# Turning two bf16 channels as one 4-byte element on VectorE, in a chunk attention followed by a multiplicative feed-forward layer

## The chip, the cores and the metric

One core of a Trainium2 chip runs the kernel. The time is the device's microseconds from start to end of one execution, and each figure is the median of several runs on one chip, except for the three single runs with other steps. Runs of one kernel lie within about 1% of each other. Each experiment is compared with runs of the kernel before beside it, on the same chip. All comparisons are of fast runs (in the single runs the state is unknown), and the profiled executions have the TensorE clock at 0.99 to 1.00 of full speed except where the text says otherwise.

## The reference, cut to what matters

```python
# q, k, v: (8, 8, 576, 64) float32: batch, heads, sequence, channels
q_c, k_c, v_c = (t.reshape(B, H, 9, 64, 64) for t in (q, k, v))       # chunks of 64
scores = matmul(q_c, k_c.transpose(0, 1, 2, 4, 3)) / sqrt(64)
attn = softmax(scores)
x = matmul(attn, v_c) -> (B * S, H * D) = (4608, 512)
h = ((x @ w1) * (x @ w2)) @ w3          # w1, w2: (512, 1024), w3: (1024, 1024)
out = h @ w_out                         # w_out: (1024, 512)
```

The kernel computes in bf16 with float32 sums, and multiplies w3 by w_out first.

## The kernel before

The 4608 tokens are 18 "pairs" of 256. For a pair, q and k have to be turned so that channels lie on partitions (T), scores are made (S), exponentials taken on ScalarE (E), multiplied by v (P), normalised (N), and the result x turned (X), again on VectorE. Then come the products with w1 and w2 (A, B), their product (C, M) and the last product (O). Two pairs share their A and B from pair 4 on. A list names the order of all these steps. W is the product of w3 (turned in V) and w_out. The kernel turns blocks of 32x32 on VectorE, so 64 channels of a head come to lie as two halves `e` on the same 32 partitions:

```python
def do_T(p, s, h=None):                                    # q (s=0) and k (s=1)
    nc.vector.transpose(
        qkT_t[g][:, :, p % 2, s].rearrange("p e h (y t) -> p h t e y", t=2),
        qk_t[p][:, s].rearrange("p h (t e y) -> p h t e y", t=2, e=2))

def do_G(g, a):                                            # pairs 8 to 17 alone: both halves
    for i in (0, 2, 1, 3):                                 # to 64 partitions, by DMA
        e = (i + a) % 2
        move(qkm_t[g][blk[i // 2 * 2 + e], i % 2], qkT_t[g][blk[i], e])

def do_S(p):
    for h in range(H):
        if p < 8:                                          # two sums over 32 channels: 64 matmuls
            for e in range(2):
                for i in range(4):
                    mm(s_t[p][...], lhsT=qkT_t[g][blk[i], e, m, 1, h, :],
                       rhs=qkT_t[g][blk[i], e, m, 0, h, :], start=(e == 0), stop=(e == 1))
        else:                                              # one sum over 64 channels: 32 matmuls
            for i in (0, 3, 1, 2):
                mm(s_t[p][...], lhsT=qkm_t[g][half[i // 2], i % 2, m, 1, h, :], rhs=..., ...)

def do_AB(p, j, f, which):
    rhs = new_xt(p // 2)[:].rearrange("p (s o t) -> p o s t", s=2, o=4)     # p >= 8
    for ki in range(4):
        mm(ps_t[p, j][:, which, ...], lhsT=w[:, ki, f * 128:(f + 1) * 128], rhs=rhs[:, ki], ...)
# ... (cut: loads, softmax, X, H, C, M, V, W, O, stores)
```

The softmax here doesn't subtract the row's maximum and nothing guards it: scores larger than these inputs give would overflow.

Of the kernel before, what the change touches and what calls it, by code (L numbers as in the profile page):

```python
# [14 lines left out]
M2.1 A2.2 N3.0 B2.2 C2.2 X3.0 A2.3 N3.1 B2.3 X3.1 C2.3 M2.2 S4 M2.3 A3.0 E4 B3.0 C3.0 A3.1 M3.0 B3.1  # L15
C3.1 V0 A3.2 M3.1 B3.2 C3.2 V1 A3.3 M3.2 B3.3 C3.3 V2 W0 M3.3 V3 W1 Z0 V4 V5 W2 Z1 V6 V7 T5.0 Z2 W3
T5.1 q10 k10 T6.0 T6.1 P4 v10 q11 k11 Z3 S5 N4.0 O0 E5 X4.0 N4.1 X4.1 T7.0 O1 T7.1 Y0 Q0 T8.0 P5 v11
q12 k12 Y1 S6 T8.1 O2 Q1 E6 N5.0 X5.0 N5.1 X5.1 O3 T9.0 T9.1 Y2 G4.0 P6 v12 q13 k13 A4.0 N6.0 B4.0
G4.1 Y3 X6.0 N6.1 C4.0 A4.1 X6.1 B4.1 C4.1 M4.0 Q2 S7 Q3 M4.1 A4.2 E7 T10.0 B4.2 C4.2 T10.1 P7 v13
q14 k14 A4.3 M4.2 B4.3 N7.0 C4.3 A4.4 X7.0 M4.3 B4.4 C4.4 N7.1 A4.5 M4.4 B4.5 C4.5 X7.1 S8 M4.5 S9  # L20
E8 A4.6 T11.0 B4.6 E9 T11.1 P8 v14 q15 k15 C4.6 A4.7 M4.6 G5.0 B4.7 C4.7 N8.0 A6.0 M4.7 B6.0 N8.1
C6.0 G5.1 A6.1 X8.0 B6.1 M6.0 C6.1 X8.1 P9 v15 A6.2 M6.1 N9.0 B6.2 C6.2 N9.1 A6.3 M6.2 B6.3 C6.3
X9.0 A6.4 M6.3 B6.4 C6.4 X9.1 A6.5 T12.0 H4.0 B6.5 C6.5 M6.4 A6.6 M6.5 B6.6 T12.1 H4.1 C6.6 S10 S11
M6.6 E10 A6.7 T13.0 B6.7 E11 P10 T13.1 C6.7 O4 M6.7 G6.0 N10.0 N10.1 X10.0 G6.1 P11 Y4 X10.1 O5
N11.0 N11.1 x11 q16 k16 v16 Q4 X11.0 X11.1 T14.0 A8.0 H5.0 Y5 B8.0 T14.1 C8.0 A8.1 M8.0 B8.1 H5.1
C8.1 T15.0 A8.2 B8.2 M8.1 C8.2 T15.1 Q5 A8.3 B8.3 C8.3 M8.2 G7.0 S12 M8.3 S13 E12 A8.4 T16.0 B8.4
E13 G7.1 P12 T16.1 C8.4 A8.5 B8.5 M8.4 C8.5 N12.0 A8.6 M8.5 B8.6 C8.6 N12.1 x12 q17 k17 v17 A8.7
M8.6 B8.7 C8.7 X12.0 P13 M8.7 A10.0 X12.1 B10.0 C10.0 N13.0 A10.1 M10.0 B10.1 N13.1 C10.1 A10.2
X13.0 B10.2 M10.1 C10.2 X13.1 S14 S15 M10.2 E14 A10.3 H6.0 T17.0 B10.3 E15 P14 T17.1 C10.3 A10.4
H6.1 M10.3 B10.4 C10.4 N14.0 A10.5 M10.4 B10.5 G8.0 C10.5 N14.1 A10.6 M10.5 B10.6 C10.6 X14.0 P15  # L30
G8.1 X14.1 A10.7 M10.6 B10.7 N15.0 C10.7 O6 N15.1 M10.7 X15.0 X15.1 H7.0 S16 Y6 S17 O7 E16 E17 H7.1
P16 Y7 O8 Q6 N16.0 Q7 N16.1 X16.0 X16.1 P17 Y8 A12.0 N17.0 Q8 B12.0 N17.1 C12.0 A12.1 X17.0 B12.1
M12.0 C12.1 X17.1 A12.2 M12.1 H8.0 B12.2 C12.2 A12.3 M12.2 B12.3 C12.3 H8.1 A12.4 M12.3 B12.4 C12.4
A12.5 M12.4 B12.5 C12.5 A12.6 M12.5 B12.6 C12.6 A12.7 M12.6 B12.7 C12.7 O9 M12.7 O10 Y9 Q9 A14.0 Y10
B14.0 C14.0 Q10 A14.1 M14.0 B14.1 C14.1 A14.2 M14.1 B14.2 C14.2 A14.3 M14.2 B14.3 C14.3 A14.4 M14.3
B14.4 C14.4 A14.5 M14.4 B14.5 C14.5 A14.6 M14.5 B14.6 C14.6 A14.7 M14.6 B14.7 C14.7 O11 M14.7 O12
Y11 Q11 A16.0 Y12 B16.0 C16.0 Q12 A16.1 M16.0 B16.1 C16.1 A16.2 M16.1 B16.2 C16.2 A16.3 M16.2 B16.3
C16.3 A16.4 M16.3 B16.4 C16.4 A16.5 M16.4 B16.5 C16.5 A16.6 M16.5 B16.6 C16.6 A16.7 M16.6 B16.7
C16.7 O13 M16.7 O14 Y13 Q13 O15 Y14 Q14 O16 Y15 Q15 Y16 Q16 O17
"""  # L40


# [1 line left out]
def kernel(  # L44
# [11 lines left out]
    nc = tc.nc  # L56
    B, H, S, D = q.shape
    P = 128
    BL = 32
    NB = P // BL  # L60
    CH = 64
# [3 lines left out]
    DF = moe_w1.shape[1]  # L65
    KO = DM // P
    FO = DF // P
    UT = 2 * CH
    PT = 2 * UT
# [6 lines left out]
    bf = mybir.dt.bfloat16  # L76
    f32 = mybir.dt.float32
# [5 lines left out]
    asb = ctx.enter_context(tc.tile_pool(name="asb", bufs=2))  # L83
    msb = ctx.enter_context(tc.tile_pool(name="msb", bufs=2))
    ps = ctx.enter_context(tc.tile_pool(name="ps", bufs=4, space=bass.MemoryType.PSUM))

    def inorder(ins):
        tc.keep_in_program_order(ins)
        return ins

    def mm(*a, **kw):
        return inorder(nc.tensor.matmul(*a, **kw))  # L92

    def load(dst, src):
        return inorder(nc.gpsimd.dma_start(dst, src))  # L95

    def psum(name):
        return ps.tile([P, 2, 512], f32, tag="p", name=name)


    w1 = wpool.tile([P, KO, DF], bf, name="w1")
    w2 = wpool.tile([P, KO, DF], bf, name="w2")

    w3 = wpool.tile([P, DF // BL, DF // NB], bf, name="w3")
    wo = wpool.tile([P, FO, DM], bf, name="wo")
# [20 lines left out]
    qk_t = {}  # L126
# [15 lines left out]
    def heads(h):  # L142
        return slice(0, H) if h is None else slice(h * HH, (h + 1) * HH)
# [31 lines left out]

    def load_wo():
        for i in range(NB):
            load(wo[i * BL:(i + 1) * BL],
                 moe_w_out[i * DF // NB:(i + 1) * DF // NB].rearrange("(k x) n -> x k n", x=BL))

    half = [slice(0, CH), slice(CH, P)]
    blk = [slice(i * BL, (i + 1) * BL) for i in range(NB)]
    qkT_t, qkm_t, s_t, e_t, pv_t, xn_t, xm_t, xt_t = {}, {}, {}, {}, {}, {}, {}, {}
# [7 lines left out]
    def do_T(p, s, h=None):  # L191


        g = p // 2
        if g not in qkT_t:
            qkT_t[g] = asb.tile([P, 2, 2, 2, H, CH], bf, tag="qkT", bufs=2, name="qkT")
        inorder(nc.vector.transpose(  # L197
            qkT_t[g][:, :, p % 2, s, heads(h)].rearrange("p e h (y t) -> p h t e y", t=2),
            qk_t[p][:, s, heads(h)].rearrange("p h (t e y) -> p h t e y", t=2, e=2)))
# [10 lines left out]
    def do_S(p, hh=None):  # L210
        g, m = divmod(p, 2)
        if p not in s_t:
            s_t[p] = psum("s_ps")
        for h in range(H)[heads(hh)]:
            if p < 8:
                for e in range(2):
                    for i in range(NB):
                        mm(s_t[p][half[i % 2], i // 2, h * CH:(h + 1) * CH],
                           lhsT=qkT_t[g][blk[i], e, m, 1, h, :], rhs=qkT_t[g][blk[i], e, m, 0, h, :],
                           start=(e == 0), stop=(e == 1))  # L220
            else:
                for i in (0, 3, 1, 2):
                    mm(s_t[p][half[i % 2], i // 2, h * CH:(h + 1) * CH],
                       lhsT=qkm_t[g][half[i // 2], i % 2, m, 1, h, :],
                       rhs=qkm_t[g][half[i // 2], i % 2, m, 0, h, :], start=True, stop=True)
# [35 lines left out]

    def new_xt(g):

        if g not in xt_t:
            xt_t[g] = asb.tile([P, KO * GT], bf, tag="xt", bufs=4, name="xt")
        return xt_t[g]

    def do_X(p, u):
        g, m = divmod(p, 2)
        if p < 8:  # L270
            t0 = m * PT + u * UT
            inorder(nc.vector.transpose(  # L272
                new_xt(g)[:].rearrange("p (o t) -> p o t", o=KO)[:, :, t0:t0 + UT]
                .rearrange("p o (m y) -> p m o y", y=BL),
                xn_t[p][:, u].rearrange("p r (c n) (z o) -> p (r c) o n z", c=2, o=KO)))
        else:

            if g not in xm_t:
                xm_t[g] = asb.tile([P, 2, KO, 2, UT], bf, tag="xm", bufs=2, name="xm")
            inorder(nc.vector.transpose(  # L280
                xm_t[g][:, u, :, m].rearrange("p o (c y) -> p c o y", y=BL),
                xn_t[p][:].rearrange("p u r m d -> p (u r) m d")[:, :, 2 * u:2 * u + 2]
                .rearrange("p c n (z o) -> p c o n z", o=KO)))

    def do_H(g, a):

# [4 lines left out]
    ab_t, ps_t, a_t, o_t = {}, {}, {}, {}  # L291
# [9 lines left out]
    def do_AB(p, j, f, which):  # L301

        if p >= 8:
            rhs = new_xt(p // 2)[:].rearrange("p (s o t) -> p o s t", s=2, o=KO)
        else:
            rhs = new_xt(p // 2)[:].rearrange("p (o t) -> p o t", o=KO)
            if p < 4:
                rhs = rhs[:, :, p % 2 * PT:(p % 2 + 1) * PT]
        fs = (f,) if p >= 4 else (2 * j, 2 * j + 1)
        n = GT // len(fs)  # L310
        for i, f in enumerate(fs):
            for ki in range(KO):
                mm(ps_t[p, j][:, which, i * n:(i + 1) * n],
                   lhsT=(w1, w2)[which][:, ki, f * P:(f + 1) * P], rhs=rhs[:, ki],
                   start=(ki == 0), stop=(ki == KO - 1))

    def do_A(p, j):
# [3 lines left out]
    def do_B(p, j):  # L321
        do_AB(p, j, j, 1)
# [55 lines left out]
    w3T_t = {}  # L378

    def do_V(f):  # L380
        w3T_t[f] = msb.tile([P, FO, P], bf, tag="w3T", bufs=4, name="w3T")
        inorder(nc.vector.transpose(
            w3T_t[f][:].rearrange("p k (f y) -> p f k y", y=BL),
            w3[:, NB * f:NB * (f + 1), :].rearrange("p f (k x) -> p f k x", x=BL)))

    def do_W(m):
        ps_t["w", m] = psum("w_ps")
        for i in range(2):
            w3T = w3T_t.pop(2 * m + i)
            for ki in range(FO):  # L390
                mm(ps_t["w", m][:, i, :], lhsT=w3T[:, ki, :], rhs=wo[:, ki, :],
                   start=(ki == 0), stop=(ki == FO - 1))

    def do_Z(m):
# [59 lines left out]
```

## Time and profile before

| | before |
|---|---|
| median | 245 us (244.5 to 245.5) |
| TensorE busy, share of the span | 93% |
| VectorE busy | 153.7 us |
| instruction packets of TensorE's queue | 21 |

A row of the table of groups by shape has line, engine, operation and tiles, then the count, busy us and mean ns of one, then idle time before. The mean ns of a matmul is its modelled duration and not its pace, as matmuls overlap: the first row has a mean of 379 ns, while the same matmuls follow one another every 216 ns. The pace is read from the chain or the timeline: a stretch divided by its count. These rows of the kernel before are the ones to compare with later, first the groups and then four pieces of the chain of waits (start us, us, what):

```profile
L92 PE MATMUL ab_ps<-xt,w 128*128 128x512 bf16 x441 | 99.2, 379 | 0.5
L92 PE MATMUL ab_ps<-xt,w 128*128 128x256 bf16 x240 | 27.6, 273 | 0.9 <-DVE xt L272 0.9
L92 PE MATMUL s_ps<-qkm 64*64 64x64 bf16 x320 | 3.6, 194 | 0.0
```

```profile
44.14 0.64 PE s_ps L92 x64
96.43 0.64 PE s_ps L92 x64
98.90 0.37 PE pv L92 x30
188.06 13.81 PE ab_ps L92 x64
```

The last line gives the pace of a 128x512 matmul of x: 13.81 us / 64 = 216 ns. The line at 96.43 us is the scores of two pairs, 32 matmuls each.

### The profile page before, as it was taken

The page shows a single profiled execution, that of the slowest core. Times are in us where ns is not written, and L with a number is a line of the kernel's source. Part 1 is how long each engine was busy: PE and PEld are TensorE (multiplying, and loading weights), DVE is VectorE, ACT ScalarE, POOL GpSimd, SP SyncE. Part 2 cuts the span into 40 slices and gives each one's busy share as a digit, 9 for nine tenths or more (in the row PEclk, how much of TensorE's full clock was granted, in tenths as well). Part 3 has the DMA queues.
Part 4 walks back from the last instruction along what each step waited for, and adds up shares of the span by engine and source line. Part 5 has one row for each costly group of instructions (what it writes and reads, how often), then busy time and mean ns, then how long its engine had stood idle before and what let it go on. Part 6 is the DMA issues. An engine that isn't in the chain of part 4 may idle for free.

```text
span 243.1 us, 6347 instructions
## 1 busy us (share of the span) xinstructions
PE 225.9 (93%) x2731; PEld 120.3 (49%) x2753; DVE 153.7 (63%) x232; ACT 85.1 (35%) x116; POOL 83.3 (34%) x112
## 2 busy tenths in 40 slices
PE   1299989999999979999999999999999999999994
PEld 1247868864545444444444444444444444444443
DVE  1856799689899578999998899918440332143000
ACT  2412323423333343534326335162332332332322
POOL 8847974665986444773260240000000000000000
PEclk9999999999999999999999999999999999999999
DMA  7999999999999999999999893735502200400244
GB/s 179 179 185 180 186 168 199 196 193 170 154 172 218 226 228 252 173 219 192 209 237 213 251 137 83 173 89 203 145 0 89 86 0 0 175 0 1 86 173 173
DMA packets 93595, 37.63 MB, mean 155 GB/s; under 512 B 75008, under 2 KB 86528, under 8 KB 93568
## 3 DMA queue, kind: packets, MB, share of 16 engines
q0 software_dynamic: 82592, 18.88, 83.9%
q1 hardware_dynamic: 9936, 17.83, 24.8%
q10 hardware_dynamic: 1040, 0.52, 0.8%
q8 instruction: 21, 0.34, 0.6%
q14 instruction: 6, 0.05, 0.1%
HBM read 38.80 MB, written 9.44 MB: 198 GB/s over the span
## 4 chain that ended last, share of the span: by engine, by line
PE 70%; DMA 16%; DVE 5%; SPq 3%; issue 2%; POOL 2%; ACT 0%; DVEq 0%; POOLq 0%
PE ab_ps L92 38%; PE o_ps L92 23%; PE w_ps L92 6%; DMA w<-in_moe_w_dram 4%; DMA qkm<-qkT 3%; DMA xt<-xm 3%; DMA qk<-in_k_dram 3%; DMA qk<-in_q_dram 3%; SPq L189 3%; PE s_ps L92 2%; PE pv L92 2%; DVE qkT L197 2%; DVE xn L260 1%; DVE ab L341 1%; POOL vbuf L95 1%
## 5 line engine op out<-in xcount | busy, mean ns | idle before, releaser
L92 PE MATMUL ab_ps<-xt,w 128*128 128x512 bf16 (+1 forms) x681 | 126.8, 342 | 1.4 <-DVE xt L272 0.9
L92 PEld LDWEIGHTS <-w 128*128 128x128 bf16 x704 | 67.3, 98 | 55.4 <-DVE xt L272 1.4
L341 DVE TENSOR_TENSOR ab<-a_sb,ab_ps 128x512 bf16<-128x512 f32 x71 | 47.8, 674 | 43.5 <-ACT a_sb L326 43.3
L326 ACT COPY a_sb<-ab_ps 128x512 f32<-128x512 f32 x71 | 41.6, 586 | 81.3 <-PE ab_ps L92 81.1
L92 PE MATMUL o_ps<-w3o,ab 128*128 128x512 bf16 (+1 forms) x285 | 63.3, 373 | 0.6
L197 DVE STREAM_TRANSPOSE qkT<-qk 128x1024 bf16<-128x1024 bf16 x36 | 45.1, 1289 | 8.0 <-ACT qk L140 5.5
L92 PEld LDWEIGHTS <-ab 128*128 128x128 bf16 x296 | 28.5, 98 | 32.3
L95 POOL DMA_DIRECT2D vbuf<-in_v_dram x40 | 33.9, 855 | 17.9 <-DMA qk<-in_k_dram 4.8
L371 ACT COPY o_sb<-o_ps 128x1024 f32<-128x1024 f32 x17 | 17.2, 1012 | 45.2 <-PE o_ps L92 41.3
L260 DVE TENSOR_TENSOR xn<-pv,rc 128x512 bf16<-128x512 f32 x36 | 24.9, 692 | 1.4
L95 POOL DMA_DIRECT2D qk<-in_q_dram x23 | 18.1, 790 | 9.9 <-DMA qk<-in_k_dram 3.1
L95 POOL DMA_DIRECT2D qk<-in_k_dram x23 | 18.0, 785 | 8.8 <-DMA vbuf<-in_v_dram 5.1
L230 ACT ACTIVATE e<-s_ps 128x1024 bf16<-128x1024 f32 x16 | 15.9, 1028 | 2.5 <-PE s_ps L92 2.2
L92 PE MATMUL w_ps<-wo,w3T 128*128 128x512 bf16 x62 | 13.9, 379 | 0.1
L280 DVE STREAM_TRANSPOSE xm<-xn 128x512 bf16<-128x512 bf16 x20 | 13.6, 697 | 0.2
L257 DVE RECIPROCAL rc<-pv 128x8 f32<-128x8 f32 x36 | 6.9, 192 | 9.9 <-PE pv L92 9.9
L95 POOL DMA_DIRECT2D w<-in_moe_w_dram x16 | 11.1, 697 | 5.8 <-DMA vbuf<-in_v_dram 2.3
L92 PEld LDWEIGHTS <-e 64*32 64x32 bf16 (+1 forms) x832 | 7.8, 97 | 8.5 <-issue 7.1
L272 DVE STREAM_TRANSPOSE xt<-xn 128x512 bf16<-128x512 bf16 x16 | 11.4, 711 | 0.5
L92 PE MATMUL pv<-vbuf,e 64*32 64x65 bf16 (+1 forms) x832 | 10.2, 198 | 1.5 <-ACT e L230 1.1
L92 PEld LDWEIGHTS <-qkT 32*64 32x64 bf16 x512 | 5.5, 117 | 11.0 <-DVE qkT L197 7.9
L364 DVE COPY o_sb<-o_ps 128x256 f32<-128x256 f32 x1 | 0.4, 425 | 16.0 <-PE o_ps L92 16.0
(24 smaller groups left out, 52.9 us busy)
## 6 DMA issues: line engine op xcount, KB each, us to landing
out_dram<-o_sb SPq DMA_DIRECT2D x17, 512.0 KB, 3.2
qkm<-qkT SPq DMA_DIRECT2D x40, 128.0 KB, 4.6
vbuf<-in_v_dram POOLq DMA_DIRECT2D x32, 128.0 KB, 8.6
w<-in_moe_w_dram POOLq DMA_DIRECT2D x16, 256.0 KB, 9.6
qk<-in_q_dram POOLq DMA_DIRECT2D x11, 256.0 KB, 6.9
qk<-in_k_dram POOLq DMA_DIRECT2D x11, 256.0 KB, 7.5
xt<-xm SPq DMA_DIRECT2D x40, 64.0 KB, 3.2
wo<-in_moe_w_out_dram POOLq DMA_DIRECT2D x4, 256.0 KB, 8.4
```

Of the source, the lines that this page charges most:

```text
L92: return inorder(nc.tensor.matmul(*a, **kw))
L95: return inorder(nc.gpsimd.dma_start(dst, src))
L189: inorder(nc.sync.dma_start(dst, src))
L197: inorder(nc.vector.transpose(qkT_t[g][:, :, p % 2, s, heads(h)].rearrange("p e h (y t) -> p h t e y", t=2), qk_t[p][:, s, heads(h)].rearr ...
L230: inorder(nc.scalar.activation(e_t[p][:, :, heads(hh)], s_t[p][:].rearrange("p u (h q) -> p u h q", q=CH)[:, :, heads(hh)], Exp, scale=sca ...
L257: inorder(nc.vector.reciprocal(rc[:], pv[:, :, :, D:W]))
L260: inorder(nc.vector.tensor_mul(xn_t[p][:, u], pv[:, :, :, 0:D], rc.to_broadcast([P, 2, 4, D])))
L272: inorder(nc.vector.transpose(new_xt(g)[:].rearrange("p (o t) -> p o t", o=KO)[:, :, t0:t0 + UT] .rearrange("p o (m y) -> p m o y", y=BL), ...
L280: inorder(nc.vector.transpose(xm_t[g][:, u, :, m].rearrange("p o (c y) -> p c o y", y=BL), xn_t[p][:].rearrange("p u r m d -> p (u r) m d" ...
L326: inorder(nc.scalar.copy(a_t[p, j][:], ps_t[p, j][:, 0, :]))
L341: inorder(nc.vector.tensor_mul(o, view(a_t.pop((p, j))[:]), view(ps_t.pop((p, j))[:, 1, :])))
L371: inorder(nc.scalar.copy(o_sb[:], ps_t.pop(p)[:]))
```

## The change

Its intent is to halve VectorE's transposes. Two neighbouring bf16 channels are handed over as one 4-byte element, so that half as many elements are turned. The two channels then stay side by side behind each token, and TensorE reads every second element. For q and k the pair of channels stays on its partition, the halves `e` are neighbours, and pairs 8 to 17 go without the transfers qkm and take the 32x64 score tiles of the others.

```diff
 def do_T(p, s, h=None):
-    qkT_t[g] = asb.tile([P, 2, 2, 2, H, CH], bf, ...)
+    qkT_t[g] = asb.tile([P, 2, 2, H, CH, 2], bf, ...)
+    nc.vector.transpose(
+        qkT_t[g][:, p % 2, s].rearrange("p h y e -> p h (y e)").bitcast(f32)
+        .rearrange("p h (y t) -> p h t y", t=2),
+        qk_t[p][:, s].bitcast(f32).rearrange("p h (t y) -> p h t y", t=2))
 def do_S(p, hh=None):
-            if p < 8:
+            if p < 18:
-                           lhsT=qkT_t[g][blk[i], e, m, 1, h, :], rhs=qkT_t[g][blk[i], e, m, 0, h, :],
+                           lhsT=qkT_t[g][blk[i], m, 1, h, :, e], rhs=qkT_t[g][blk[i], m, 0, h, :, e],
 def do_X(p, u):                            # x, the same for both layouts
-                xn_t[p][:, u].rearrange("p r (c n) (z o) -> p (r c) o n z", c=2, o=KO)
+                xn_t[p][:, u].bitcast(f32).rearrange("p r (c n) (z o) -> p (r c) o n z", c=2, o=KO // 2)
 def do_AB(p, j, f, which):
-            rhs = new_xt(p // 2)[:].rearrange("p (s o t) -> p o s t", s=2, o=KO)
+            rhs = new_xt(p // 2)[:].rearrange("p (s a t b) -> p a b s t", s=2, a=KO // 2, b=2)
-                   ... rhs=rhs[:, ki]
+                   ... rhs=rhs[:, ki // 2, ki % 2]
# cut: w3 in the same way (V, W), the load of w_out in its new row order, and the order of steps
# without G4.0 to G8.1
```

More of the change, by code (lines that the diff above doesn't have):

```diff
@@ L17 @@
 T5.1 q10 k10 T6.0 T6.1 P4 v10 q11 k11 Z3 S5 N4.0 O0 E5 X4.0 N4.1 X4.1 T7.0 O1 T7.1 Y0 Q0 T8.0 P5 v11
-q12 k12 Y1 S6 T8.1 O2 Q1 E6 N5.0 X5.0 N5.1 X5.1 O3 T9.0 T9.1 Y2 G4.0 P6 v12 q13 k13 A4.0 N6.0 B4.0
-G4.1 Y3 X6.0 N6.1 C4.0 A4.1 X6.1 B4.1 C4.1 M4.0 Q2 S7 Q3 M4.1 A4.2 E7 T10.0 B4.2 C4.2 T10.1 P7 v13
-q14 k14 A4.3 M4.2 B4.3 N7.0 C4.3 A4.4 X7.0 M4.3 B4.4 C4.4 N7.1 A4.5 M4.4 B4.5 C4.5 X7.1 S8 M4.5 S9
-E8 A4.6 T11.0 B4.6 E9 T11.1 P8 v14 q15 k15 C4.6 A4.7 M4.6 G5.0 B4.7 C4.7 N8.0 A6.0 M4.7 B6.0 N8.1
@@ L22 @@
-C6.0 G5.1 A6.1 X8.0 B6.1 M6.0 C6.1 X8.1 P9 v15 A6.2 M6.1 N9.0 B6.2 C6.2 N9.1 A6.3 M6.2 B6.3 C6.3
-X9.0 A6.4 M6.3 B6.4 C6.4 X9.1 A6.5 T12.0 H4.0 B6.5 C6.5 M6.4 A6.6 M6.5 B6.6 T12.1 H4.1 C6.6 S10 S11
-M6.6 E10 A6.7 T13.0 B6.7 E11 P10 T13.1 C6.7 O4 M6.7 G6.0 N10.0 N10.1 X10.0 G6.1 P11 Y4 X10.1 O5
-N11.0 N11.1 x11 q16 k16 v16 Q4 X11.0 X11.1 T14.0 A8.0 H5.0 Y5 B8.0 T14.1 C8.0 A8.1 M8.0 B8.1 H5.1
-C8.1 T15.0 A8.2 B8.2 M8.1 C8.2 T15.1 Q5 A8.3 B8.3 C8.3 M8.2 G7.0 S12 M8.3 S13 E12 A8.4 T16.0 B8.4
-E13 G7.1 P12 T16.1 C8.4 A8.5 B8.5 M8.4 C8.5 N12.0 A8.6 M8.5 B8.6 C8.6 N12.1 x12 q17 k17 v17 A8.7
@@ L28 @@
-M8.6 B8.7 C8.7 X12.0 P13 M8.7 A10.0 X12.1 B10.0 C10.0 N13.0 A10.1 M10.0 B10.1 N13.1 C10.1 A10.2
-X13.0 B10.2 M10.1 C10.2 X13.1 S14 S15 M10.2 E14 A10.3 H6.0 T17.0 B10.3 E15 P14 T17.1 C10.3 A10.4
-H6.1 M10.3 B10.4 C10.4 N14.0 A10.5 M10.4 B10.5 G8.0 C10.5 N14.1 A10.6 M10.5 B10.6 C10.6 X14.0 P15
-G8.1 X14.1 A10.7 M10.6 B10.7 N15.0 C10.7 O6 N15.1 M10.7 X15.0 X15.1 H7.0 S16 Y6 S17 O7 E16 E17 H7.1
-P16 Y7 O8 Q6 N16.0 Q7 N16.1 X16.0 X16.1 P17 Y8 A12.0 N17.0 Q8 B12.0 N17.1 C12.0 A12.1 X17.0 B12.1
-M12.0 C12.1 X17.1 A12.2 M12.1 H8.0 B12.2 C12.2 A12.3 M12.2 B12.3 C12.3 H8.1 A12.4 M12.3 B12.4 C12.4
@@ L34 @@
-A12.5 M12.4 B12.5 C12.5 A12.6 M12.5 B12.6 C12.6 A12.7 M12.6 B12.7 C12.7 O9 M12.7 O10 Y9 Q9 A14.0 Y10
-B14.0 C14.0 Q10 A14.1 M14.0 B14.1 C14.1 A14.2 M14.1 B14.2 C14.2 A14.3 M14.2 B14.3 C14.3 A14.4 M14.3
-B14.4 C14.4 A14.5 M14.4 B14.5 C14.5 A14.6 M14.5 B14.6 C14.6 A14.7 M14.6 B14.7 C14.7 O11 M14.7 O12
-Y11 Q11 A16.0 Y12 B16.0 C16.0 Q12 A16.1 M16.0 B16.1 C16.1 A16.2 M16.1 B16.2 C16.2 A16.3 M16.2 B16.3
-C16.3 A16.4 M16.3 B16.4 C16.4 A16.5 M16.4 B16.5 C16.5 A16.6 M16.5 B16.6 C16.6 A16.7 M16.6 B16.7
@@ L39 @@
-C16.7 O13 M16.7 O14 Y13 Q13 O15 Y14 Q14 O16 Y15 Q15 Y16 Q16 O17
+q12 k12 Y1 S6 T8.1 O2 Q1 E6 N5.0 X5.0 N5.1 X5.1 O3 T9.0 T9.1 Y2 P6 v12 q13 k13 A4.0 N6.0 B4.0 Y3
+X6.0 N6.1 C4.0 A4.1 X6.1 B4.1 C4.1 M4.0 Q2 S7 Q3 M4.1 A4.2 E7 T10.0 B4.2 C4.2 T10.1 P7 v13 q14 k14
+A4.3 M4.2 B4.3 N7.0 C4.3 A4.4 X7.0 M4.3 B4.4 C4.4 N7.1 A4.5 M4.4 B4.5 C4.5 X7.1 S8 M4.5 S9 E8 A4.6
+T11.0 B4.6 E9 T11.1 P8 v14 q15 k15 C4.6 A4.7 M4.6 B4.7 C4.7 N8.0 A6.0 M4.7 B6.0 N8.1 C6.0 A6.1 X8.0
+B6.1 M6.0 C6.1 X8.1 P9 v15 A6.2 M6.1 N9.0 B6.2 C6.2 N9.1 A6.3 M6.2 B6.3 C6.3 X9.0 A6.4 M6.3 B6.4
@@ new lines @@
+C6.4 X9.1 A6.5 T12.0 H4.0 B6.5 C6.5 M6.4 A6.6 M6.5 B6.6 T12.1 H4.1 C6.6 S10 S11 M6.6 E10 A6.7 T13.0
+B6.7 E11 P10 T13.1 C6.7 O4 M6.7 N10.0 N10.1 X10.0 P11 Y4 X10.1 O5 N11.0 N11.1 x11 q16 k16 v16 Q4
+X11.0 X11.1 T14.0 A8.0 H5.0 Y5 B8.0 T14.1 C8.0 A8.1 M8.0 B8.1 H5.1 C8.1 T15.0 A8.2 B8.2 M8.1 C8.2
+T15.1 Q5 A8.3 B8.3 C8.3 M8.2 S12 M8.3 S13 E12 A8.4 T16.0 B8.4 E13 P12 T16.1 C8.4 A8.5 B8.5 M8.4 C8.5
+N12.0 A8.6 M8.5 B8.6 C8.6 N12.1 x12 q17 k17 v17 A8.7 M8.6 B8.7 C8.7 X12.0 P13 M8.7 A10.0 X12.1 B10.0
@@ new lines @@
+C10.0 N13.0 A10.1 M10.0 B10.1 N13.1 C10.1 A10.2 X13.0 B10.2 M10.1 C10.2 X13.1 S14 S15 M10.2 E14
+A10.3 H6.0 T17.0 B10.3 E15 P14 T17.1 C10.3 A10.4 H6.1 M10.3 B10.4 C10.4 N14.0 A10.5 M10.4 B10.5
+C10.5 N14.1 A10.6 M10.5 B10.6 C10.6 X14.0 P15 X14.1 A10.7 M10.6 B10.7 N15.0 C10.7 O6 N15.1 M10.7
+X15.0 X15.1 H7.0 S16 Y6 S17 O7 E16 E17 H7.1 P16 Y7 O8 Q6 N16.0 Q7 N16.1 X16.0 X16.1 P17 Y8 A12.0
+N17.0 Q8 B12.0 N17.1 C12.0 A12.1 X17.0 B12.1 M12.0 C12.1 X17.1 A12.2 M12.1 H8.0 B12.2 C12.2 A12.3
+M12.2 B12.3 C12.3 H8.1 A12.4 M12.3 B12.4 C12.4 A12.5 M12.4 B12.5 C12.5 A12.6 M12.5 B12.6 C12.6 A12.7
@@ new lines @@
+M12.6 B12.7 C12.7 O9 M12.7 O10 Y9 Q9 A14.0 Y10 B14.0 C14.0 Q10 A14.1 M14.0 B14.1 C14.1 A14.2 M14.1
+B14.2 C14.2 A14.3 M14.2 B14.3 C14.3 A14.4 M14.3 B14.4 C14.4 A14.5 M14.4 B14.5 C14.5 A14.6 M14.5
+B14.6 C14.6 A14.7 M14.6 B14.7 C14.7 O11 M14.7 O12 Y11 Q11 A16.0 Y12 B16.0 C16.0 Q12 A16.1 M16.0
+B16.1 C16.1 A16.2 M16.1 B16.2 C16.2 A16.3 M16.2 B16.3 C16.3 A16.4 M16.3 B16.4 C16.4 A16.5 M16.4
+B16.5 C16.5 A16.6 M16.5 B16.6 C16.6 A16.7 M16.6 B16.7 C16.7 O13 M16.7 O14 Y13 Q13 O15 Y14 Q14 O16
+Y15 Q15 Y16 Q16 O17
@@ L177, in load_wo @@
         for i in range(NB):
-            load(wo[i * BL:(i + 1) * BL],
-                 moe_w_out[i * DF // NB:(i + 1) * DF // NB].rearrange("(k x) n -> x k n", x=BL))
+            load(wo[i * BL:(i + 1) * BL].rearrange("p (k e) n -> p k (e n)", e=2),
+                 moe_w_out[i * DF // NB:(i + 1) * DF // NB].rearrange("(k x e) n -> x k (e n)", x=BL, e=2))
     half = [slice(0, CH), slice(CH, P)]
@@ L195, in do_T @@
         if g not in qkT_t:
-            qkT_t[g] = asb.tile([P, 2, 2, 2, H, CH], bf, tag="qkT", bufs=2, name="qkT")
+            qkT_t[g] = asb.tile([P, 2, 2, 2, H, CH] if p >= 18 else [P, 2, 2, H, CH, 2], bf,
+                                tag="qkT", bufs=2, name="qkT")
+        if p < 18:
+            inorder(nc.vector.transpose(
+                qkT_t[g][:, p % 2, s, heads(h)].rearrange("p h y e -> p h (y e)").bitcast(f32)
+                .rearrange("p h (y t) -> p h t y", t=2),
+                qk_t[p][:, s, heads(h)].bitcast(f32).rearrange("p h (t y) -> p h t y", t=2)))
+            return
         inorder(nc.vector.transpose(
@@ L214, in do_S @@
         for h in range(H)[heads(hh)]:
-            if p < 8:
+            if p < 18:
                 for e in range(2):
@@ L272, in do_X @@
             inorder(nc.vector.transpose(
-                new_xt(g)[:].rearrange("p (o t) -> p o t", o=KO)[:, :, t0:t0 + UT]
+                new_xt(g)[:].bitcast(f32).rearrange("p (o t) -> p o t", o=KO // 2)[:, :, t0:t0 + UT]
                 .rearrange("p o (m y) -> p m o y", y=BL),
-                xn_t[p][:, u].rearrange("p r (c n) (z o) -> p (r c) o n z", c=2, o=KO)))
+                xn_t[p][:, u].bitcast(f32).rearrange("p r (c n) (z o) -> p (r c) o n z", c=2, o=KO // 2)))
         else:
             if g not in xm_t:
-                xm_t[g] = asb.tile([P, 2, KO, 2, UT], bf, tag="xm", bufs=2, name="xm")
+                xm_t[g] = asb.tile([P, 2, KO // 2, 2, 2 * UT], bf, tag="xm", bufs=2, name="xm")
             inorder(nc.vector.transpose(
-                xm_t[g][:, u, :, m].rearrange("p o (c y) -> p c o y", y=BL),
-                xn_t[p][:].rearrange("p u r m d -> p (u r) m d")[:, :, 2 * u:2 * u + 2]
-                .rearrange("p c n (z o) -> p c o n z", o=KO)))
+                xm_t[g][:, u, :, m].bitcast(f32).rearrange("p o (c y) -> p c o y", y=BL),
+                xn_t[p][:].bitcast(f32).rearrange("p u r m d -> p (u r) m d")[:, :, 2 * u:2 * u + 2]
+                .rearrange("p c n (z o) -> p c o n z", o=KO // 2)))
     def do_H(g, a):
@@ L303, in do_AB @@
         if p >= 8:
-            rhs = new_xt(p // 2)[:].rearrange("p (s o t) -> p o s t", s=2, o=KO)
+            rhs = new_xt(p // 2)[:].rearrange("p (s a t b) -> p a b s t", s=2, a=KO // 2, b=2)
         else:
-            rhs = new_xt(p // 2)[:].rearrange("p (o t) -> p o t", o=KO)
+            rhs = new_xt(p // 2)[:].rearrange("p (a t b) -> p a b t", a=KO // 2, b=2)
             if p < 4:
-                rhs = rhs[:, :, p % 2 * PT:(p % 2 + 1) * PT]
+                rhs = rhs[:, :, :, p % 2 * PT:(p % 2 + 1) * PT]
         fs = (f,) if p >= 4 else (2 * j, 2 * j + 1)
@@ L313, in do_AB @@
                 mm(ps_t[p, j][:, which, i * n:(i + 1) * n],
-                   lhsT=(w1, w2)[which][:, ki, f * P:(f + 1) * P], rhs=rhs[:, ki],
+                   lhsT=(w1, w2)[which][:, ki, f * P:(f + 1) * P], rhs=rhs[:, ki // 2, ki % 2],
                    start=(ki == 0), stop=(ki == KO - 1))
@@ L380, in do_V @@
     def do_V(f):
-        w3T_t[f] = msb.tile([P, FO, P], bf, tag="w3T", bufs=4, name="w3T")
+        w3T_t[f] = msb.tile([P, FO // 2, P, 2], bf, tag="w3T", bufs=4, name="w3T")
         inorder(nc.vector.transpose(
-            w3T_t[f][:].rearrange("p k (f y) -> p f k y", y=BL),
-            w3[:, NB * f:NB * (f + 1), :].rearrange("p f (k x) -> p f k x", x=BL)))
+            w3T_t[f][:].rearrange("p k y e -> p k (y e)").bitcast(f32).rearrange("p k (f y) -> p f k y", y=BL),
+            w3[:, NB * f:NB * (f + 1), :].bitcast(f32).rearrange("p f (k x) -> p f k x", x=BL)))
     def do_W(m):
@@ L390, in do_W @@
             for ki in range(FO):
-                mm(ps_t["w", m][:, i, :], lhsT=w3T[:, ki, :], rhs=wo[:, ki, :],
+                mm(ps_t["w", m][:, i, :], lhsT=w3T[:, ki // 2, :, ki % 2], rhs=wo[:, ki, :],
                    start=(ki == 0), stop=(ki == FO - 1))
```

## The prediction

Its times for 1024 and 512 elements are those of the 2-byte transposes on VectorE in the trace of the kernel before.

> **What bounds the kernel now.** I read the page's busy shares first, then the 40 slices, the table of stretches, the groups by shape, the chain of waits in order of time, and last the list of DMA packets. Busy shares and slices:
>
> ```profile
> PE 225.9 (93%) x2731; PEld 120.3 (49%) x2753; DVE 153.7 (63%) x232; ACT 85.1 (35%) x116; POOL 83.3 (34%) x112
> PE   1299989999999979999999999999999999999994
> DVE  1856799689899578999998899918440332143000
> q8 instruction: 21, 0.34, 0.6%
> ```
>
> TensorE is at 9 tenths from the third slice on, so VectorE's 63% is beside it. As busy matmuls can still be slow ones, I took the stretches (PE, PEld, DVE busy, number of instructions):
>
> ```profile
> 20.00:30.00 10.00, 9.67 (x162) 8.21 (x148) 8.51 (x13) 3.52 (x6) 8.64 (x11) 1.00 1.81 180
> 50.00:60.00 10.00, 9.95 (x56) 5.34 (x55) 10.00 (x11) 3.20 (x4) 5.63 (x8) 1.00 1.81 181
> 210.00:220.00 10.00, 10.00 (x48) 4.50 (x47) 3.65 (x6) 3.52 (x6) 0.00 (x0) 1.00 0.15 54
> ```
>
> In 50 to 60 us VectorE is busy all 10.00 us and TensorE still loses 0.05; in 210 to 220 us VectorE has 3.65 us of work and TensorE loses nothing. The start-to-start time of the 128x512 matmuls is 216 ns in both. After 20 us TensorE idles 4 us in all (the stretches' sum), plus some 3 us behind its last matmul. The pieces of the chain that are not TensorE's steady work:
>
> ```profile
> 30.40 1.32 DVE qkT L197
> 33.15 0.71 DVE xt L272
> 34.72 0.72 DVE xt L272
> 35.48 1.92 PE ab_ps L92 x16
> ...
> 86.45 0.53 PE s_ps L92 x51
> 86.98 1.40 issue
> 88.38 0.31 PE s_ps L92 x13
> ```
>
> The first four lines are a true VectorE wait: TensorE stands 0.55 us before 35.48. The last three are something else. In the middle of a score burst of pair 7, after 51 of 64 matmuls, TensorE stops for 1.40 us, and the matmul that follows waits for no semaphore. In the packet list a 16 KB instruction packet runs from 85.58 to 86.88 us, and TensorE resumes 1.5 us after its end. The same picture, smaller, is at 30.4 us (0.40 us of idle, "issue"). I read both as TensorE waiting for its own instructions.
>
> [...] 1024 elements take 1217 to 1289 ns, 512 take 697 to 711, about 1.0 to 1.1 ns an element plus 180 ns. No 4-byte transpose is in it. [...]
>
> **The change part by part.**
>
> VectorE rows of before:
>
> ```profile
> L197 DVE STREAM_TRANSPOSE qkT<-qk 128x1024 bf16<-128x1024 bf16 x36 | 45.1, 1289 | 8.0 <-ACT qk L140 5.5 <-DMA qk<-in_q_dram 1.3 <-PE s_ps L92 0.9
> L280 DVE STREAM_TRANSPOSE xm<-xn 128x512 bf16<-128x512 bf16 x20 | 13.6, 697 | 0.2
> L382 DVE STREAM_TRANSPOSE w3T<-w 128x1024 bf16<-128x1024 bf16 x8 | 9.4, 1217 | 1.7 <-DMA w<-in_moe_w_dram 1.7
> ```
>
> With half the elements I expect about 710 ns for q and k (saves 36 x 0.58 = 21 us), 440 ns for x (36 x 0.26 = 9.4 us) and 700 ns for w3 (8 x 0.5 = 4 us): VectorE falls from 154 to about 120 us. Nearly all of it lies beside TensorE.
>
> What reaches TensorE's path is at the start. S0 begins when the second q/k transpose ends, at 9.54 us; the casts on ScalarE end at 7.9 us, so two halved transposes let it start about 0.8 us earlier. At 23.5 us TensorE stands 0.5 us and at 34.6 us 0.6 us for xt, both gone. That would be 1.9 us. But loads take most of it back. From the semaphores' times, the second half of the last w1/w2 quarter lands at 28.95 us, and its first weight load ran at 29.1 us: only 0.15 us of slack. What is won before ends there. Then q of pair 3 lands at 30.4 us. From there the shorter transposes save 0.6 + 2 x 0.26 us of the chain, more than the 0.55 us wait. So I count 0.5 us, not 1.9.
>
> Removed: 40 transfers qkm<-qkT of 128 KB. The one wait they could explain is 0.2 us, at 139.2 us. I count 0.2 us, and 0.5 us for a shorter instruction wait at 87 us, because the first eight of these transfers, issued from 80 to 84.5 us, no longer stand with the instruction packet in the queues.
>
> Added on TensorE. Ten pairs go from 32 matmuls on 64x64 to 64 on 32x64 tiles. The group of two pairs in 64x64 is 64 matmuls from 96.36 to 97.00, 0.64 us, of which about 0.12 us is the change to the next stage; one pair in 32x64 at 44.14 us is also 64 matmuls in 0.64 us. So one matmul costs 8.2 ns in both, whatever its rows: 10 x 32 x 8.2 ns = 2.6 us more, all on the path.
>
> Added instructions: 640 (320 matmuls, 320 weight loads). Stops at instruction blocks come every 256 instructions, and from the two stops I place the borders at instruction 194 of each 256. Up to pair 7 the order is unchanged. After it, borders fall 36 instructions into S8, 18 into S10, just before S12, 8 into S14. Behind each come some 220 to 250 instructions of a doubled score burst at 4 ns each, then only 8 big matmuls (1.7 us): the next border comes about 2.9, 2.9, 1.6 and 2.1 us later (before: 8.1, 14, 8.3, 8.1 us). From the border's crossing to TensorE's going on it took, in before: packet start 2.7 us (S8) and 3.3 us (S10) after the crossing, 0.9 to 1.2 us of packet, 1.4 us behind it: 5 and 6 us while loads fill the DMA; for S12 and S14 about 1.4 and 2.9 us. So waits of about 2.1, 3, 0 and 0.8 us, an estimate of 6 us. TensorE's sequencer reads ahead by an amount that I can't fix, and the removed transfers shorten the queue, so I take 3.7 us.
>
> Sum: 245.2 - 0.5 - 0.7 + 2.6 + 3.7 = 250.3 us.
>
> **The rivals.** First, the added matmuls are all that counts: the sequencer fetches early enough. For it: 19 of 21 borders cost nothing, and late ones without loads are fetched 2 us ahead. Against: the two shortest intervals of before, 4.6 and 6.2 us, both stopped, and the new ones are half as long. It makes 245.2 + 2.6 - 1.2 = 246.6 us. Second, the early savings are kept in full and the doubled bursts cost little: 1.9 + 1.2 against 2.6, 244.7 us. Against it stands the landing at 28.95 us, which no transpose moves. Third, the 4-byte step slows TensorE's reads. Some 576 matmuls of 512 columns take x strided; at half rate they would add 124 us, and a strided score burst alone perhaps 5 us. [...] I give it 6%. Fourth, 4-byte transposes are no faster: VectorE stays at 154 us, TensorE loses only the 0.5 us, 250.8 us.
>
> **Range and chances.** Without instruction waits and with a good start it is about 246; with the full 6 us and a longer wait at 87 us it is 253 to 254. So 246 to 254. The 2% border is 250.1 us, close to the middle. Faster by 2% would need 240.3 us, which nothing here offers: 0.03. Slower 0.50, within 2% 0.47.
>
> **What would show it.** VectorE's busy time near 120 us, with q/k transposes near 710 ns. 23 or 24 instruction packets. In the timeline of TensorE, score bursts of 128 matmuls of about 1.2 us, and "issue" idles of 1 to 3 us inside P8 and at P10, with a 16 KB packet ending about 1.4 us before each goes on. 128x512 matmuls still 216 ns apart: if they are further apart, the stride step is wrong. If TensorE's first x matmul of pair 2 (35.48 us) comes more than 1 us earlier, my account of the loads is wrong. If no issue idle is behind 95 us, the instruction step is wrong and the time is near 246.6.

## The result, and the profile after

The changed kernel takes 252.96 us (252.58 to 253.58), the kernel before 244.97 us (244.49 to 245.45) beside it. A ratio here is the mean of one kernel's fast runs over the mean of the other's of the same rounds, so not quite the ratio of the medians: it is 1.0328 (95% interval 1.0297 to 1.0359). The change costs 3.3%, 8.0 us.

Rows of the page after, busy us and share of the span, and two DMA queues:

```profile
PE 234.2 (93%) x3051; PEld 122.1 (49%) x3073; DVE 121.6 (48%) x232; ACT 85.5 (34%) x116; POOL 83.2 (33%) x112
q1 hardware_dynamic: 8016, 12.59, 15.4%
q8 instruction: 24, 0.39, 0.6%
```

VectorE's work fell by 32 us as meant. TensorE still fills 93% of a longer span. The groups by shape, after:

```profile
L92 PE MATMUL ab_ps<-xt,w 128*128 128x512 bf16 x441 | 103.9, 388 | 0.7 <-DVE rc L266 0.2
L92 PE MATMUL ab_ps<-xt,w 128*128 128x256 bf16 x240 | 28.4, 275 | 1.2 <-DMA w<-in_moe_w_dram 1.2
L92 PE MATMUL s_ps<-qkT 32*64 32x64 bf16 x1024 | 11.2, 193 | 0.3 <-issue 0.3
L201 DVE STREAM_TRANSPOSE qkT<-qk 128x512 f32<-128x512 f32 x36 | 24.0, 692 | 12.6 <-ACT qk L140 5.9 <-DMA qk<-in_k_dram 3.5 <-DMA qk<-in_q_dram 3.2
L290 DVE STREAM_TRANSPOSE xm<-xn 128x256 f32<-128x256 f32 x20 | 8.2, 431 | 0.3
L392 DVE STREAM_TRANSPOSE w3T<-w 128x512 f32<-128x512 f32 x8 | 5.5, 702 | 4.3 <-DMA w<-in_moe_w_dram 2.3 <-PE w_ps L92 2.0
```

The reader sees a half-length transpose on each VectorE row. In the first row the same matmuls of x (441 of 448 are recorded) have become longer, though their shape is the same. The chain of waits, after:

```profile
22.72 6.97 DMA w<-in_moe_w_dram
29.69 0.04 issue
29.73 1.08 PE ab_ps L92 x8
...
87.19 0.28 issue
...
95.86 1.20 PE s_ps L92 x128
...
98.97 0.21 PE pv L92 x10
99.18 1.43 issue
100.61 0.38 PE pv L92 x21
...
116.06 1.23 PE s_ps L92 x128
...
164.18 1.53 PE s_ps L92 x128
...
195.34 14.50 PE ab_ps L92 x64
```

Four things are in it. (1) The last line: 64 matmuls of x take 14.50 us in place of 13.81, 227 ns each in place of 216; the single start-to-start times have this as their median, over the whole run. (2) The scores of two pairs take 1.20 us in place of 0.64. (3) In P8 TensorE stops for 1.43 us by "issue", which means that the profile shows nothing that it waited for, as it did for 1.40 us in S7 before; in S7 it is now 0.28. (4) The first three lines: TensorE waits for a quarter of w1 and w2 that lands at 29.69 us, whatever it won before. The product W starts at 51.7 us in both traces: of the earlier start (S0 at 8.94 in place of 9.54 us) nothing is left there.

I took two theories to the chip. The first was that the new step of two elements in x slows the matmuls themselves, and that this and the scores of pairs 8 to 17 each make about half of the loss. The rival was my prediction's: the step is harmless, and the loss is the longer bursts of scores and the waits for instructions.

### The profile page after: what moved, and what is told of

The parts are those of the page before. It is cut to its first block, busy times and chain, and to the rows that moved or that the text cites. A ratio compares the mean times of both kernels' runs of the same rounds, so it can differ in the third digit from the quotient of the medians.

```text
span 251.8 us, 6918 instructions
## 1 busy us (share of the span) xinstructions
PE 234.2 (93%) x3051; PEld 122.1 (49%) x3073; DVE 121.6 (48%) x232; ACT 85.5 (34%) x116; POOL 83.2 (33%) x112
## 4 chain that ended last, share of the span: by engine, by line
PE 86%; DMA 10%; issue 2%; POOL 1%; DVE 0%; DVEq 0%; POOLq 0%
PE ab_ps L92 49%; PE o_ps L92 25%; DMA w<-in_moe_w_dram 7%; PE w_ps L92 5%; PE s_ps L92 4%; PE pv L92 3%; DMA qk<-in_k_dram 3%; POOL vbuf L95 1%; POOL qk L95 0%; POOL w L95 0%; DVE o_sb L374 0%; DVE rc L266 0%; DVEq L374 0%; POOLq L448 0%
## 5 line engine op out<-in xcount | busy, mean ns | idle before, releaser
L92 PE MATMUL ab_ps<-xt,w 128*128 128x512 bf16 (+1 forms) x681 | 132.3, 348 | 2.0 <-DMA w<-in_moe_w_dram 1.2
L92 PEld LDWEIGHTS <-w 128*128 128x128 bf16 x704 | 66.1, 96 | 62.4 <-DMA w<-in_moe_w_dram 1.6
L351 DVE TENSOR_TENSOR ab<-a_sb,ab_ps 128x512 bf16<-128x512 f32 x71 | 48.5, 683 | 68.2 <-ACT a_sb L336 68.1
L201 DVE STREAM_TRANSPOSE qkT<-qk 128x512 f32<-128x512 f32 x36 | 24.0, 692 | 12.6 <-ACT qk L140 5.9
L92 PEld LDWEIGHTS <-qkT 32*64 32x64 bf16 x1152 | 11.6, 110 | 11.6 <-DVE qkT L201 6.9
L92 PE MATMUL s_ps<-qkT 32*64 32x64 bf16 x1024 | 11.2, 193 | 0.3 <-issue 0.3
L92 PEld LDWEIGHTS <-w3T 128*128 128x128 bf16 x64 | 6.2, 97 | 7.4
```

The lines of the kernel that those rows point to most:

```text
L92: return inorder(nc.tensor.matmul(*a, **kw))
L201: inorder(nc.vector.transpose(qkT_t[g][:, p % 2, s, heads(h)].rearrange("p h y e -> p h (y e)").bitcast(f32) .rearrange("p h (y t) -> p h ...
L351: inorder(nc.vector.tensor_mul(o, view(a_t.pop((p, j))[:]), view(ps_t.pop((p, j))[:, 1, :])))
```

## The experiments

Ten kernels ran. All but the three with other steps and the one with unit steps give the reference's result.

**Reading x in unit steps.** Everything of the changed kernel stays; only the order in which A and B read x from pair 4 on is other, and the result is wrong on purpose.

```diff
-        if p >= 8:
-            rhs = new_xt(p // 2)[:].rearrange("p (s a t b) -> p a b s t", s=2, a=KO // 2, b=2)
+        if p >= 4:
+            rhs = new_xt(p // 2)[:].rearrange("p (s a b t) -> p a b s t", s=2, a=KO // 2, b=2)
```

> From pair 4 on TensorE reads x in unit steps where the changed kernel reads every second bf16 element; nothing else differs, and the result is wrong on purpose. Step theory (a 128x512 matmul of x takes 227 ns instead of 216 because its moving operand has a step of two elements): 448 such matmuls get back to 216 ns, some 4.8 us, so about 248.2 us. Rival (the slower matmuls come from something else that changed, such as what VectorE writes or what the queues carry at that time): they stay at 227 ns and the time at 253 us.

It took 248.63 us, ratio to before 1.0173 (1.0129 to 1.0217). One piece of its chain:

```profile
191.59 13.81 PE ab_ps L92 x64
```

The pace is back at 216 ns by the reading order alone, with VectorE's 4-byte writes and the queues left as they are. The rival falls: the step is the cause of the slower matmuls. By the ratios the time is 3.8 us below the changed kernel's, where 4.8 were expected; the two intervals together leave about 1.3 us of doubt.

**The x part alone, on the kernel before.** The functions X and A/B of the changed kernel, in the kernel before.

```diff
 # in the kernel before: do_X and do_AB of the change, nothing else
+    xm_t[g] = asb.tile([P, 2, KO // 2, 2, 2 * UT], bf, ...)
+    rhs = new_xt(p // 2)[:].rearrange("p (s a t b) -> p a b s t", s=2, a=KO // 2, b=2)
```

> The kernel before with the x part of the change alone: x turned as 4-byte elements on VectorE, read with a step of two by TensorE. Step theory: 512-column matmuls of x at 227 ns and 256-column ones at 113 instead of 109, together 5.9 us more, less at most 0.5 us from shorter waits: about 250.4 us. Rival (the stride is harmless and the loss is the bursts and instruction waits): 245 us or a little below.

It took 249.54 us, ratio 1.0200 (1.0169 to 1.0231): 4.9 us of loss from this part alone, 0.9 us less than expected. The matmuls are at 227 and 113 ns, as expected. The wait in S7 stays at 1.23 us, so faster transposes of x did not shorten it.

**The x part undone, on the changed kernel.**

```diff
 # in the changed kernel: do_X and do_AB of the kernel before
-    rhs = new_xt(p // 2)[:].rearrange("p (s a t b) -> p a b s t", s=2, a=KO // 2, b=2)
+    rhs = new_xt(p // 2)[:].rearrange("p (s o t) -> p o s t", s=2, o=KO)
```

> The changed kernel with x turned and read as before; q, k, w3 and the 32x64 scores stay changed. Step theory: matmuls of x back at 216 and 109 ns, 5.9 us less, about 247.2 us, correct result; what is left over the kernel before is the score bursts (3.1 us) and the instruction wait in pair 8 (1.4 us), less 1 us of shorter waits. Rival (stride harmless): 253 us.

It took 248.03 us, ratio 1.0138 (1.0099 to 1.0177), 0.8 us above what was expected. Against the changed kernel's 1.0328 this is 1.9%, 4.7 us. The two ways of asking for the x part agree (each is known to about 1 us). What TensorE waited for in this run, longest first (total us, times, longest), with two lines left out:

```profile
PE z_ps L92 <- DVE qkT L201: 6.5, 1, 6.5
PE pv L92 <- issue: 1.6, 1, 1.6
PE z_ps L92 <- issue: 1.3, 1, 1.3
...
PE ab_ps L92 <- DVE xt L282: 1.0, 2, 0.7
```

The wait inside P8 is there also without the x part (1.6 us); it comes with the scores.

**Pairs 8 to 17 undone, on the changed kernel.**

```diff
-        if p < 18:
+        if p < 8:           # in T and S; 2-byte transposes and the qkm transfers above
 # and the order of steps of the kernel before, with G4.0 to G8.1
```

> The changed kernel with pairs 8 to 17 as before: 2-byte transposes, qkm transfers, 64x64 score tiles; x and w3 and pairs 0 to 7 stay changed. If the parts add: 3.1 us of score bursts, 1.4 us of instruction wait behind S8 and S9 and 0.3 us in S16 go, and up to 1.1 us of the instruction wait in S7 comes back with the qkm transfers: 248.2 to 249.6 us, and no idle by issue behind 95 us. Rival (the bursts were hidden and x is all of the loss): 252.5 us or more.

It took 248.14 us, ratio 1.0139 (1.0107 to 1.0171): 1.9%, 4.6 us, is what the change of pairs 8 to 17 costs. That is what the traces before and after give for their scores: the five bursts take 1.20, 1.23, 1.20, 1.20 and 1.53 us in place of 0.64 each, together 3.2 us, and the wait in P8 is 1.4 us. A part of the expectation missed: the qkm transfers came back, and the long wait in S7 did not. Those transfers alone do not make it.

**Both undone.** Kept are the 4-byte transposes of w3 and of q and k of pairs 0 to 7.

```diff
 # in the changed kernel: do_X and do_AB of the kernel before, and
-        if p < 18:
+        if p < 8:
```

> Only what costs TensorE nothing is kept of the change: 4-byte transposes of w3 and of q and k of pairs 0 to 7; x, and q and k of pairs 8 to 17, as before. If the parts add, it is the run with the pairs back (248.1 us) less 5.3 us: 242.8 us, some 0.8% below the kernel before, by the start (0.6 to 0.9 us) and the instruction waits at 30 and 87 us that are gone. Rival (those waits come back when x moves again, and loads eat the start): 244.6 us, the same as before.

It took 243.96 us, beside 244.92 of the kernel before, ratio 0.9951 (0.9936 to 0.9967). Within their intervals the parts add: -1.2 us for what is kept, 4.7 for x and 4.6 for the scores make 8.1 us, and the change measured 8.0. This is the version that beats both kernels, by half a per cent of the one before, so less than the 242.8 us that I had expected. Its busy times show that the rest of VectorE's savings is not needed:

```profile
PE 225.8 (93%) x2731; PEld 120.0 (50%) x2753; DVE 140.9 (58%) x232; ACT 85.0 (35%) x116; POOL 83.0 (34%) x112
```

W starts about 0.6 us earlier than in the kernel before, and S7 waits 0.34 us in place of 1.40. The span is only 1.1 us shorter; where the other half microsecond goes I did not follow.

**Moving the borders of the instruction blocks.** The dummy matmuls at the start run in TensorE's idle time: in the trace after, it waits 6.7 us for VectorE behind them. With 84 more it still waited 3.3 us there, so they delay nothing, but each adds two instructions (a weight load and a matmul) ahead of all others.

```diff
-... o h0 h1 D0.0.0.16.64 K0 T0.0 ...
+... o h0 h1 D0.0.0.100.64 K0 T0.0 ...
```

> The changed kernel with 84 more dummy matmuls in the idle time before 6.5 us: they delay nothing on the path but move every border of an instruction block 168 instructions earlier in the program. Instruction theory: the waits by issue inside S7 (0.28 us) and P8 (1.43 us) go or become less than 0.4 us together, about 251.3 us; a new one of up to 1 us can come in the score bursts of pairs 3 or 12. Rival (the 1.43 us in P8 is a wait for something else, such as a buffer): it stays in P8 and the time at 253 us.

It took 252.82 us, ratio 1.0307 (1.0286 to 1.0328), so no gain in time. But its timeline of TensorE shows what happened (start us, us, what, idle before):

```profile
43.42 0.60 PE L92 MATMUL s_ps<-qkT 32*64 32x64 bf16 x49
45.39 0.32 PE L92 MATMUL s_ps<-qkT 32*64 32x64 bf16 x15 [1.38 <-issue]
...
96.47 1.27 PE L92 MATMUL s_ps<-qkT 32*64 32x64 bf16 x128
97.67 1.98 PE L92 MATMUL ab_ps<-xt,w 128*128 128x512 bf16 x7
99.58 0.45 PE L92 MATMUL pv<-vbuf,e 64*64 64x65 bf16 x32
```

S7 and P8 run through, and a wait of 1.38 us stands in S4, where neither kernel had one; it lies on the new border, and the instruction packet for it ended 1.35 us before TensorE went on (1.4 to 1.6 us at the five waits on borders in the traces before and after). Nothing but the position in the instruction stream had changed for these steps. That settles what "issue" is here. Other traces agree: in the kernels with steps of one and two, shifted or not, every wait by issue over 0.35 us stands between instructions 184 and 194 of a block of 256 of TensorE's stream, counted by recorded instructions. The blocks fit the packets: 21 before and 24 after, 16 KB each, for some 5,560 and 6,190 instructions of TensorE. (The shift is not quite free of side effects: after the longer row of dummies S0 took 0.71 us in place of 1.06.) The expectation of 251.3 us missed because one border of the shifted stream fell into another burst (I had named those of pairs 3 and 12, not 4).

The same trick with 12 dummies more on the version that beats both:

```diff
-... o h0 h1 D0.0.0.16.64 K0 T0.0 ...
+... o h0 h1 D0.0.0.28.64 K0 T0.0 ...
```

> The run that keeps only the harmless parts (243.96 us) with 12 more dummy matmuls in the idle time before 2.9 us, which move the borders of the instruction blocks 24 instructions earlier. Instruction theory: the idle by issue inside S7 (0.28 us) goes, about 243.6 us. Rival (nothing depends on the borders): 243.96 us, S7 unchanged.

It took 245.21 us, ratio 1.0009 (0.9988 to 1.0031), a miss. S7 still waits, 0.28 us in place of 0.34, and now after 39 of its 64 matmuls in place of 51: the wait moved with the border and hardly shrank. A new one of about 1 us came in the early scores of pair 1. Moving the borders was a lottery here, with the loads in the queues; it showed the cause and made no better kernel.

**How the cost grows with the step.** The same line as in the first experiment, with steps of 4, 8 and 3 elements from pair 4 on, all wrong on purpose, one run each. In all three `p >= 8` becomes `p >= 4` as before, and the step of 3 takes `rhs[:, ki % 3]`.

```diff
-            rhs = new_xt(p // 2)[:].rearrange("p (s a t b) -> p a b s t", s=2, a=KO // 2, b=2)
+            rhs = new_xt(p // 2)[:].rearrange("p (s t a b) -> p a b s t", s=2, a=KO // 2, b=2)       # step 4
+            rhs = new_xt(p // 2)[:].rearrange("p (t a c b) -> p a b c t", a=2, b=2, c=2)             # step 8
+            rhs = new_xt(p // 2)[:, 0:3 * GT].rearrange("p (s t b) -> p b s t", s=2, b=3)            # step 3
```

> From pair 4 on, x is read with a step of four elements, 8 bytes (wrong on purpose). [...] a 512-column matmul takes about 216 + 33 = 249 ns, the run some 262 us. If it is a fixed cost for any step[...], 227 ns and 253 us.

> From pair 4 on, x is read with a step of eight elements, 16 bytes[...] (wrong on purpose). [...] about 216 + 77 = 293 ns, 282 us. [...] If no step costs more than the first: 227 ns.

> From pair 4 on, x is read with a step of three elements, 6 bytes (wrong on purpose). Runs so far: 216, 227, 453 and 900 ns for steps of 1, 2, 4 and 8. If TensorE's reads are limited by the bytes they pass over (1024 columns of 2 bytes in 227 ns, 9.0 bytes per ns and partition), a 512-column matmul takes 3072 / 9.0 = 340 ns and the run about 303 us. If only powers of two count[...], 453 ns and 352 us.

The runs took 352.2, 565.05 and 301.51 us. None of the estimates for steps 4 and 8 came near: 249 or 227 ns against 452.5, and 293 or 227 against 900. (The larger ones add 11 ns, the difference of steps 1 and 2, for each further element of the step; 227 takes every step to cost as much as that of two.) In the chain with a step of 8, 64 matmuls of x:

```profile
416.81 57.60 PE ab_ps L92 x64
```

That is 900 ns each. The median start-to-start times of all 128x512 matmuls of x:

| step, elements | bytes passed over by 512 columns | ns | bytes per ns and partition |
|---|---|---|---|
| 1 | 1024 | 216 | 4.7 |
| 2 | 2048 | 227 | 9.0 |
| 3 | 3072 | 339 | 9.1 |
| 4 | 4096 | 452.5 | 9.1 |
| 8 | 8192 | 900 | 9.1 |

The step of 3 was expected at 340 ns from the others, and came at 339. In these runs a 128x512 matmul whose moving operand (x, its `rhs`) is read in steps goes at 9.0 to 9.1 bytes passed over per ns and partition, or at the 216 ns of unit steps, whichever is slower. Up to a step of 8, which is 16 bytes, a matmul also reads from every stretch of 16 bytes or more that it passes, so these runs can't tell bytes passed over from such stretches touched; a larger step was not run. The step of two that the change brought is just over that edge: 5%. The 256-column matmuls fit too: 1024 bytes in 113 ns. In the run with a step of 8 the granted TensorE clock changed between 1.0 and 0.5, 0.64 on average. The matmuls of x are 900 ns apart in the stretches at 1.0 as in those at 0.5 (from 100 to 150 us the clock was 0.50, and 24 of them from 106.44 us on take 21.69 us, 904 ns each), so the 900 ns are not the clock's.

Not every operand suffered. The scores of pairs 0 to 7 also read q and k with a step of two in the changed kernel, and 64 of their small matmuls take 0.64 us as before (43.91 us in the chain after, 44.14 in the one before). W takes its stationary operand, the weights (w3T in the trace's weight loads), with a step of two, and 49 of its matmuls take 10.74 us in both.

## Why the prediction was right or wrong, point by point

The time, 252.96 us, was within the range of 246 to 254 and on the side called likeliest, but that was luck. The sum of 250.3 us lacked the largest cost, 4.7 us for the step in x, and came as near as it did because it had 2.3 us too much for instruction waits.

- **VectorE's savings**: right. Predicted about 710, 440 and 700 ns and 120 us in all; measured 692, 431 to 445, 702 ns and 121.6 us. A 4-byte transpose of 512 elements took 692 to 702 ns, a 2-byte one 697 to 711, so the time here went with the elements and not with the bytes.
- **The start is taken back by loads**: right in kind. TensorE waited for the last quarter of w1 and w2, which landed at 29.69 us in place of 28.95. W began no earlier. The 256-column matmuls of x cost 1.1 us more by then (256 x 4.2 ns). If this is hidden behind the same load, it explains why the x part costs 4.7 to 4.9 us and not the 6.0 of all its matmuls. The traces show it only in part: with pairs 8 to 17 as before, W starts at 51.1 us with the x part and without it; with them changed, at 51.7 and 51.0.
- **The added score matmuls**: right in kind. Predicted 2.6 us, measured 3.2, of which 0.3 are in S16 and S17 alone, for a reason that I did not follow.
- **Waits for instructions**: the mechanism was right, the size was not. Predicted 3.7 us, taken from waits of 2.1 behind S8, 3 at S10, 0 and 0.8; measured 1.43 in P8 and none at the others. I had taken the packet's delays from the kernel before. At the border in or just behind S10 the next packet started 3.3 us behind the crossing then, and 2.5 us ahead of it now. The load queue was full there before and ran dry after; queue 0 in the window from 110 to 114 us (packets, MB, and the packets' time as a share of 16 engines' span), first before, then after:

```profile
q0 software_dynamic: 2776, 0.53, 157.5%
```

```profile
q0 software_dynamic: 1244, 0.15, 60.9%
```

  The loads were that far ahead by then. In the traces before and after, the packet for a block starts from about 5 us ahead to 4.8 us behind TensorE's crossing into the block before it, so instructions are read about one block ahead. A rival is that TensorE's sequencer reads further ahead when big matmuls stand before the border, as they do in the changed kernel only. The run with 84 dummies speaks for the loads: its borders lie 0.5, 0.4 and 0.3 us into the bursts S8, S10 and S12, and the next packet starts 3.95, 0.93 and 0.93 us behind them, with the load queue full at the first (205.5% of 16 engines in the 5 us from 96 us on) and empty or nearly so at the others (0 and 13%). I did not test it with loads taken away.
- **The wait in S7**: right that it would shrink (1.40 to 0.28 us), wrong in why. The qkm transfers were named; with them back it was still gone. It stayed in the run with the x part alone, so it goes with the 4-byte q, k or w3 or the new load of w_out; in which way is open.
- **The step of two elements in x**: this is the step that failed. The prediction counted nothing for it; that the step would be free was shown by no trace or run. As a rival it considered only half rate, an estimate of mine, with 6%. The truth lay between: 227 ns in place of 216, 11 ns on 448 matmuls. Without this term, the sum of what was measured, 3.2 for scores, 1.4 for P8 and -1.2 for the rest, is 3.4 us; with 4.7 us for x it is 8.1. Mine, 5.1 us, missed 4.7 us for x and 0.6 for scores, and had 2.3 us too much for instructions.
- **The signs named beforehand** did their work: "128x512 matmuls still 216 ns apart: if they are further apart, the stride step is wrong" is what the trace showed first. Of the others, 24 packets and bursts of 1.2 us came; the first x matmul of pair 2 came 0.5 us earlier, within the limit of 1 us; the wait in P8 came, the one at P10 did not.

## What to carry to other kernels

Before a layout change that makes another engine faster, ask what the bound engine has to read afterwards: 32 us of VectorE's work went away here and brought about 1 us, while 5% on TensorE's main operand (227 ns in place of 216) cost 4.7 to 4.9 us. Check a strided matmul operand with one line in a wrong-on-purpose kernel, because the reading order is then all that the edit changes. In this kernel, which is bound by TensorE, the 320 added small matmuls cost twice, 3.2 us by their own time in the bursts and 1.4 us in P8 by the instructions that had to be fetched for them while the loads ran: count the instructions between the borders, here 256 in a packet of 16 KB. Here all waits at borders of over 0.25 us stood behind blocks of 256 whose own work took 3.2 to 6.8 us, while loads ran. Some blocks of 4.5 to 5 us ran through even then, and in the changed kernel blocks of 1.6 to 3.6 us did behind 116 us, when fewer loads ran, so this is no sharp limit.
